# One core, three chained networks: the last block's stage joined with block 3's down product, a re-costed planner, six units' numerators in float32

## Chip, cores and metric

The kernel runs on one NeuronCore of a Trainium2 chip. The metric is the device time of one execution in microseconds; of several runs the median is taken. TensorE (PE) does the matrix products, ScalarE (ACT), VectorE (DVE) and GpSimd (POOL) the elementwise work, SyncE (SP) and ACT issue the DMAs.

## The reference

Everything is float32. B = 4, H = 8, S = 576, D = 64, M = 128 features; 2304 tokens, d_model 512, d_ff 1536; then 8 experts with 4 slots each and a hidden size of 1024.

```python
# 1: attention by random features, for each (b, h)
phi(x) = exp(x @ omega.T - |x|^2/2 - rowmax) / sqrt(M)
kv, z  = phi(k).T @ v, sum_s phi(k)
att    = (phi(q) @ kv) / (phi(q) @ z + 1e-6)       # -> x, 2304 x 512
# 2: gated block
x2  = (sigmoid(x @ w_gate) * (x @ w_val)) @ w_out  # 512 -> 1536 -> 512
# 3: soft mixture of experts
logits = x2 @ phi                                  # 2304 x 32
d = softmax over the tokens; slot_input = d.T @ x2 # 32 x 512
slot_out[e] = relu(slot_input[e] @ w1[e]) @ w2[e]
c = softmax over the slots; out = c @ slot_out
```

## The kernel before, in words

**Tiling.** The heads are taken two at a time: 16 units (`u`), four per batch. The tokens of the gated block are five blocks (`BLOCKS`): blocks 0 to 3 with 512 tokens, the last one (block 4) with the 64 left-over tokens of each batch, 256 in all. d_ff is cut into 12 steps `f` of 128. Products that need more than one float32r pass are made of three: both operands are split into a float32r high part (`hi_of`, a copy) and low part (`lo_of`, a subtract), and `three` (line 464) issues high x high, high x low, low x high. Other products are plain float32 and appear in the trace as two matmul instructions each.

**Stages** (`GROUPS`, and the loop at line 1525): block 0's first six steps beside the units 4 to 7; all of block 1 beside the units 8 to 15; the rest of block 0; blocks 2 and 3 as a pair by a seven-product (Strassen-like) scheme (`pair_jobs`, line 1451), in which block 2's down product runs along and block 3's gated values are kept in `GB`; then block 3's down product alone (the tail of `pair_jobs`, 12 steps: `split_out` splits w_out's tile into w2/ga_a buffers, `late_split` splits `GB[f]`, `downs` issues 12 matmuls); then block 4 (`moe_jobs`, line 1393): for each f `gate` (line 847) 12 matmuls into bank `ga`, Sigmoid on ACT; `val` (line 861) 12 matmuls into bank `va`, a multiply on DVE, a split; `down` (line 880) 12 matmuls into `o0` to `o3`. Each step of block 4 splits three weight tiles of 128x512 (`split_w`, line 819), loaded by SP into the six slots of `WR` (trace name `ws`) from the DRAM scratch `wscr`. So w_out's tiles are loaded and split once for block 3 and once more for block 4.

**The mixture part.** When a block's x2 is done, `moe2_chunks` (line 1107) makes its logits (`chunk_logits`, 32-column matmuls), the running max and sum with Exp on ACT, transposes (`chunk_ltT`, `chunk_cT`) and the slot sums (`chunk_slot`). For the slot sums x2 is needed with tokens on the partitions: `chunk_x2` transposes 32x32 squares on DVE and `chunk_back` (line 1089) writes them into place with 16 DMAs on SP's queue (trace `x2T<-x`). `join_slots` (line 1167) joins the four row groups, `last_slots` (line 1191) adds block 4, then come `layer1` for the eight experts, `layer2` and `combine`. The expert weights (33.5 MB) are loaded into whatever region is free: w1 by `load_w1` (ACT's queue), w2 by `load_w2` (SP's queue).

**Numerators.** `chunk_num` (line 670) multiplies phi(q) by kv. For the units below `N_NUM` = 10 this is plain float32; for the units 10 to 15 kv and the transposed phi(q) are split (`chunk_kv` line 617, `chunk_qT` line 635) and `three` is used, two heads x two halves of 288 columns a unit.

**What sets the order.** Nothing is issued as written. Every operation goes into `Plan` (line 112) with a key in planned microseconds (`plan.t` less a lead by job kind, `LEAD`). The keys come from the constants `SPAN`, `SPANQ`, `SPAND`. `Plan.schedule` (line 248) then runs a list schedule: for each engine the ready operation with the lowest key, with the durations of `Plan.cost` (line 208), a hand-over `HOP` between engines, a DMA model and 1.3 us for a change of ACT's function table. A PSUM tile counts as a whole bank (`span`, line 145). The resulting order is fixed in the program: each engine runs its list in order, and waits where an operand is late. All instructions are issued by line 425 (`issue`), so the trace is read by tile names.

There are eight PSUM banks: `o0` to `o3`, `ga`, `va` and two `fl`. Trace names: `g` = the big staging regions, `XT` = tokens of a block, `gt` = split gated values, `w` = split weights, `more` and `ga_a` = further split buffers, `x` = the tag `x2`.

Of the kernel before, what the change touches and what calls it, by code (L numbers as in the profile page):

```python
# [32 lines left out]
PAIR = (2, 3)  # L33
# [28 lines left out]
N_NUM = 10  # L62
LATE8 = 0.1
FLOOR = 8
WIDE = 15
# [12 lines left out]
SPAN = [88.0, 143.0, 71.0, 45.0]  # L78
SPANQ = 147.0
SPAND = 33.0  # L80
# [5 lines left out]
    "m2": {"PE": 0, "EW": 0},  # L86
    "ex": {"PE": 0.0, "EW": 20.0, "lazy": True},
# [4 lines left out]

SIZE = {F32: 4, F32R: 4, I32: 4, U32: 4, I64: 8}
HOP = 0.16
RELOAD = 1.3
TURN = 0.2
# [5 lines left out]
class Eng:  # L102
# [5 lines left out]
    def __getattr__(self, method):  # L108
        return lambda *a, **k: self.plan.add([(self.name, method, a, k)])


class Plan:
# [95 lines left out]
    def cost(self, eng, method, kw, outs, ins):  # L208


        if method == "together":
# [3 lines left out]
        if eng == "ACT" and method == "dma_start" and o.tensor.name.startswith("out_"):  # L215
            return 0.55, False
# [28 lines left out]
        return 0.6 if eng == "SP" and o.tensor.name.startswith("x2T") and o.ap[0][1] == 32 else 0.06, False  # L245


    def schedule(self):
# [47 lines left out]
        table = 0  # L296
        order = []
# [60 lines left out]
        while ev:  # L358
# [13 lines left out]
            for e in E:  # L372
                while free_at[e] <= now + 1e-9:
# [22 lines left out]
                    want = {AF.Exp: 0, AF.Ln: 0, AF.Sigmoid: 1}.get(alt[3].get("func"), table) if e == "ACT" else table  # L396
                    if want != table:
                        c, table = c + RELOAD, want
                    if held:
                        port = now + c  # L400
                    end = now + c
                    if alt[1] == "dma_start":
# [5 lines left out]
                        end = max(dma, now + nb / 340e3) + 2.0  # L408
# [23 lines left out]
def body(ctx, tc, nc, qkT, tok, von, omT, wall, phi, w1, w2, ident_d, srep_d, rrep_d, mask_d, out):  # L432
# [330 lines left out]
    USE = [(i + (p < 2), p) for i in range(LAST - 1, NS) for p in range(3) if LAST <= i + (p < 2) < NS]  # L763
# [3 lines left out]
    def load_part(k):  # L767
        if todo:
            m = todo.pop(0)
            slot[USE[m]] = k  # L770
            W[USE[m]] = WR[:, k, :]
            SP.dma_start(out=W[USE[m]], in_=wscr[USE[m][0] % NF][:, USE[m][1], :])
# [46 lines left out]
    def split_w(i, part):  # L819
        if i >= NS:  # L820
            return
        end = (i, part) == (NS - 1, 2)
        t = T([128, 2, 512], "w0" if end else f"w{part}", F32R)
        w = W.pop((i, part))
        hi_of(t[:, 0, :], w, SITE["hw"])
        lo_of(t[:, 1, :], w, t[:, 0, :], ("DVE",) if end else SITE["lw"])
        WS[i, part] = t
        if i >= LAST:
            k = slot[i, part]
            if k < 4 or USE.index((i, part)) < WIDE:  # L830
                load_part(k)
            else:
                spent.append(k)
                if len(spent) == 2:
                    free_early()

    def up_passes(i, part, tag):
# [3 lines left out]
        ps = bank(tag)[:, 0:n]  # L841
# [5 lines left out]
    def gate(i):  # L847
        n = BLOCKS[STEPS[i][0]][1]
        ps = up_passes(i, 0, "ga")
        a = T([128, 512], "ga_a", F32, 2)[:, 0:n]  # L850
        if i >= LAST:
# [9 lines left out]
    def val(i, sg):  # L861
        n = BLOCKS[STEPS[i][0]][1]
        ps = up_passes(i, 1, "va")
        if i < LAST:
            gt = T([128, 2, 512], "gt", F32R, 2)
        else:
            if i == LAST:
                G["last"] = T([128, 2, 2, 256], "gt", F32R, 2)
# [139 lines left out]
    def evac_out(j, banks):  # L1008
        n = BLOCKS[j][1]
        x = ms["x2T"] if j == NB - 1 else T([128, 4, 512], "x2T")  # L1010
# [5 lines left out]
        if j == NB - 1:  # L1016
            x = x.rearrange("p k c -> p (k c)")[:, 0:1024].rearrange("p (k c) -> p k c", k=4)
# [4 lines left out]
    def chunk_logits(j):  # L1022
# [7 lines left out]
        lt = T([128, 2, 128], "lt", F32, 2)  # L1030
        mx = T([128, 4], "mx2", F32, 2)
# [62 lines left out]

    def chunk_slot(j):
# [3 lines left out]
        for g in range(ng):  # L1099
            PE.matmul(ps[32 * g:32 * g + 32, :].rearrange("p (c a) -> p c a", a=32), s["dt"][:, 32 * g:32 * g + 32],  # L1100
                      s["x2v"][:, g], start=True, stop=True)
# [5 lines left out]
    def moe2_chunks(j):  # L1107
        back = [lambda h=h: chunk_back(j, h) for h in range(4)]
# [15 lines left out]
    def load_w1():  # L1124

        e = len(W1)
        if e < E:
            W1.append(pieces(EXTAGS[e], 3 if EXTAGS[e] == "XT" else 1))
            for c in range(4):
                ACT.dma_start(out=W1[e][c], in_=w1[e, :, 1024 * c:1024 * c + 1024])  # L1130
# [8 lines left out]
    def free_more():  # L1139

        free.extend(pieces("more", 1, 2))
        plan.floor = plan.t
        load_w2()
        plan.floor = 0.0

    def free_early():

        lead, plan.lead = plan.lead, LEAD["ex"]
        free.append(WR[:, 4:6, :].rearrange("p a c -> p (a c)"))
# [3 lines left out]
    def free_halves():  # L1153

        ms["x2T"], ms["x2"] = T([128, 4, 512], "x2T"), T([128, 4, 512], "x2")
        for x in (ms["x2T"], ms["x2"]):
            free.append(x.rearrange("p k c -> p (k c)")[:, 1024:2048])
        load_w2()

    def free_rest():  # L1160

        w = [WR[:, k:k + 2, :].rearrange("p a c -> p (a c)") for k in (0, 2)]
        free.extend(w[:1] + pieces("w1", 1, 1) + pieces("XT4", 1, 2) + w[1:])
        for tag, bufs in (("w2", 1), ("w0", 1), ("gt", 2)):
# [26 lines left out]
    def last_slots():  # L1191
# [52 lines left out]
        free.extend([x.rearrange("p k c -> p (k c)"), x2[:, 0:2, :].rearrange("p k c -> p (k c)")])  # L1244
# [16 lines left out]
    def layer1(e, si):  # L1261

        ps = bank(("ga", "va")[e % 2])[:, 0:256]
        for k in range(4):
            for g in range(4):
                PE.matmul(ps[32 * g:32 * g + 32, :], si[:, k, :], W1[e][k][:, 256 * g:256 * g + 256],
                          start=k == 0, stop=k == 3)
# [75 lines left out]
    ACT.preload_act_table_set("natural_log_exp_and_others")  # L1343
# [107 lines left out]
    def pair_jobs(t):  # L1451
# [8 lines left out]
        def tiles():  # L1460
            g = region(0, F32)
            h = half_region(0, F32)
            GB.extend(x[:, 512 * k:512 * k + 512] for x, n in ((g, 8), (h, 4)) for k in range(n))
# [34 lines left out]
        t += SPANQ  # L1498
        places = [4, 2, 0, 4, 2, 4]
        dt = SPAND / NF  # L1500
        for n in range(6):
            f, at, t0 = 2 * n, places[n], t + SPAND * n / 6
            if n in (0, 1):
                add(t + 0.2 + 0.1 * n, lambda f=f, at=places[n + 1]: pair_load(f + 2, 2, at))
            add(t0 + 0.02, lambda f=f, at=at: (split_out(f, at), late_split(f)))
            add(t0 + 0.03, lambda f=f, at=at: (split_out(f + 1, at)))
            downs(f, t0 + 0.04 + dt, PAIR[1], "b")
            add(t0 + 0.05 + dt, lambda f=f: late_split(f + 1))
            downs(f + 1, t0 + 0.06 + 2 * dt, PAIR[1], "b")
            nxt = {0: lambda: pair_load(6, 2, 4), 1: lambda: pair_load(8, 2, 2), 3: lambda: pair_load(10, 2, 4),  # L1510
                   2: lambda: (load_part(0), load_part(1)), 4: lambda: (load_part(2), load_part(3)),
                   5: lambda: (load_part(4), load_part(5))}[n]
            add(t0 + 0.035, nxt)
        add(t + SPAND - 6.0, lambda: (split_w(LAST, 0), split_w(LAST, 1)))
        return t + SPAND

    def m2_jobs(j, t, span):
        m2c = moe2_chunks(j)
        jobs.extend((t + span * k / len(m2c), "m2", c) for k, c in enumerate(m2c))
# [5 lines left out]
    for g, (j, f0, f1) in enumerate(GROUPS):  # L1525
        span = SPAN[g]
        if j == NB - 1:
# [3 lines left out]
            jobs += [(start - SPAND + 1.0 + 8 * k, "ex", load_w1) for k in range(4)]  # L1531
            m2_jobs(PAIR[0], start - SPAND + 1.0, SPAND * 0.9)
            m2_jobs(PAIR[1], start + span / NF, span * 0.7)
            jobs += [(start - 5.0, "ex", load_w1), (start + 2.0, "ex", load_w1), (start + 8.0, "ex", free_more),
                     (start + span * 0.9, "end", free_halves), (start + span * 0.85, "m2", join_slots)]
# [10 lines left out]
    jobs += moe_jobs(NS, start, 1.0)  # L1546
# [88 lines left out]
```

## Time and profile before

| | us |
|---|---|
| median of 3 runs | 669.89 (667.93 to 673.65) |
| the profiled execution, whole time | 666.81 |
| its span, first to last instruction | 664.9 |
| PE busy | 644.0 (97%) |
| DVE / ACT / POOL busy | 479.7 / 410.6 / 289.2 |

The span is what the profile's rows divide up; 1.9 us lie around it. The profiled execution is 3.1 us shorter than the median of the three timed runs. "Busy" of PE means that some matmul was under way; as matmuls overlap by a drain of some 0.16 us, the start of one group to the start of the next is the better measure of what a group costs. The TensorE clock was granted in full (1.00, the 2.4 GHz level) in all stretches up to 655 us.

### The profile page before, as it was taken

The page shows a single profiled execution, that of the slowest core. Times are in us where ns is not written, and L with a number is a line of the kernel's source. Part 1 is how long each engine was busy: PE and PEld are TensorE (multiplying, and loading weights), DVE is VectorE, ACT ScalarE, POOL GpSimd, SP SyncE. Part 2 cuts the span into 40 slices and gives each one's busy share as a digit, 9 for nine tenths or more (in the row PEclk, how much of TensorE's full clock was granted, in tenths as well). Part 3 has the DMA queues.
Part 4 walks back from the last instruction along what each step waited for, and adds up shares of the span by engine and source line. Part 5 has one row for each costly group of instructions (what it writes and reads, how often), then busy time and mean ns, then how long its engine had stood idle before and what let it go on. Part 6 is the DMA issues. An engine that isn't in the chain of part 4 may idle for free.

```text
span 664.9 us, 12634 instructions
## 1 busy us (share of the span) xinstructions
PE 644.0 (97%) x4268; PEld 513.2 (77%) x4268; DVE 479.7 (72%) x1379; ACT 410.6 (62%) x937; POOL 289.2 (43%) x272
## 2 busy tenths in 40 slices
PE   7899999999999999999999999999999999899995
PEld 5676777768888888888877778878888779899663
DVE  5898989888998765667689987557557757756323
ACT  4899989889998866777675654534442225445012
POOL 0456344455445344455453555555551453542100
PEclk9999999999999999999999999999999999999998
DMA  7987857678976345223315552222228899777988
GB/s 233 324 269 260 274 188 273 204 237 272 298 260 215 101 115 176 90 97 98 109 49 185 195 147 78 63 64 63 65 65 293 278 316 346 229 233 264 353 334 240
DMA packets 55216, 132.17 MB, mean 199 GB/s; under 512 B 6256, under 2 KB 14192, under 8 KB 55152
## 3 DMA queue, kind: packets, MB, share of 16 engines
q1 hardware_dynamic: 49328, 114.01, 52.7%
q10 hardware_dynamic: 5824, 17.37, 7.7%
q8 instruction: 33, 0.54, 0.3%
q14 instruction: 31, 0.25, 0.1%
HBM read 113.00 MB, written 14.16 MB: 191 GB/s over the span
## 4 chain that ended last, share of the span: by engine, by line
PE 84%; DMA 5%; DVE 4%; ACT 2%; POOL 1%; SPq 1%; issue 1%; DVEq 0%; POOLq 0%; ACTq 0%
PE o L425 24%; PE fl L425 23%; PE va L425 19%; PE ga L425 18%; DMA g<-in_tok 2%; DMA x2T<-x 1%; DMA g<-in_w 1%; DVE g L425 1%; DMA ws<-wscr 1%; SPq L425 1%; DVE XT L425 1%; POOL g L425 1%; DVE ga_a L425 1%; ACT w L425 0%; DMA g<-in_qkT 0%
## 5 line engine op out<-in xcount | busy, mean ns | idle before, releaser
L425 POOL TENSOR_TENSOR w<-ws,w 128x512 fp32r<-128x512 f32 (+1 forms) x101 | 120.6, 1195 | 161.3 <-ACT w L425 67.2
L425 PE MATMUL o<-gt,w 128*128 128x512 f32 (+1 forms) x576 | 134.7, 372 | 2.2 <-POOL w L425 0.9
L425 PEld LDWEIGHTS o<-gt,w 128*128 128x128 f32 x576 | 97.2, 189 | 24.4 <-issue 2.4
L425 PE MATMUL ga<-XT,w 128*128 128x512 f32 (+1 forms) x432 | 101.6, 367 | 0.9 <-POOL XT L425 0.9
L425 ACT ACTIVATE w<-ws 128x512 fp32r<-128x512 f32 (+1 forms) x100 | 57.7, 579 | 72.3 <-PE o L425 28.1
L425 PE MATMUL va<-XT,w 128*128 128x512 f32 (+1 forms) x432 | 100.1, 366 | 1.6 <-DVE ga_a L425 1.1
L425 PE MATMUL fl<-g,g 64*128 64x128 f32 (+4 forms) x686 | 84.1, 313 | 3.5 <-ACT g L425 1.7
L425 ACT ACTIVATE g<-g 128x128 f32<-128x128 f32 (+4 forms) x206 | 73.8, 414 | 16.9 <-DVE g L425 12.9
L425 PEld LDWEIGHTS ga<-XT,w 128*128 128x128 f32 x432 | 69.9, 189 | 16.8 <-issue 4.7
L425 PEld LDWEIGHTS va<-XT,w 128*128 128x128 f32 x432 | 70.5, 189 | 15.2 <-issue 2.4
L425 PEld LDWEIGHTS fl<-g,g 64*128 64x128 f32 (+2 forms) x686 | 60.3, 182 | 24.4 <-issue 7.3
L425 ACT ACTIVATE x2T<-g 128x512 f32<-128x512 f32 x72 | 45.8, 666 | 4.2 <-DVE x L425 2.4
L425 ACT ACTIVATE g1b<-g1b,g 128x128 f32<-128x128 f32 x128 | 40.8, 389 | 5.9 <-DVE g L425 5.7
L425 DVE TENSOR_SCALAR x2T<-x2T 128x512 f32<-128x512 f32 (+1 forms) x72 | 35.9, 513 | 3.7 <-ACT x2T L425 3.4
L425 POOL TENSOR_TENSOR g<-g 128x640 f32<-128x640 f32 (+1 forms) x19 | 23.4, 1230 | 33.3 <-DMA g<-in_tok 13.3
L425 DVE CUSTOM_DVE_ANT_0 g<-fl,g 128x128 f32<-128x128 f32 x142 | 32.3, 286 | 6.5 <-PE fl L425 6.4
L425 PE MATMUL o<-gt,ga_a 128*128 128x512 f32 x144 | 35.4, 393 | 0.0
L425 DVE TENSOR_TENSOR XT<-fl,XT 128x512 f32<-128x512 f32 x24 | 16.6, 690 | 23.0 <-PE fl L425 23.0
L425 POOL TENSOR_TENSOR x<-x2T 128x512 int32<-128x512 int32 x19 | 24.6, 1295 | 16.1 <-DVE x2T L425 11.3
L425 PEld LDWEIGHTS o<-gt,ga_a 128*128 128x128 f32 x144 | 26.7, 188 | 5.8 <-POOL ga_a L425 0.3
L425 ACT ACTIVATE ga_a<-ga_a 128x512 f32<-128x512 f32 x48 | 30.0, 624 | 1.7 <-DVE ga_a L425 1.4
L425 POOL TENSOR_TENSOR w<-x,w 128x512 fp32r<-128x512 f32 x15 | 19.3, 1285 | 24.2 <-DVE x2T L425 11.5
(254 smaller groups left out, 1264.3 us busy)
## 6 DMA issues: line engine op xcount, KB each, us to landing
ws<-wscr SPq DMA_DIRECT2D x42, 512.0 KB, 3.7
g<-in_wall SPq DMA_DIRECT2D x36, 512.0 KB, 5.0
ws<-wscr SPq DMA_DIRECT2D x54, 256.0 KB, 3.7
wscr<-x SPq DMA_DIRECT2D x36, 256.0 KB, 4.6
g<-in_qkT SPq DMA_DIRECT2D x15, 576.0 KB, 5.3
g<-in_tok SPq DMA_DIRECT2D x15, 576.0 KB, 5.1
g<-in_w ACTq DMA_DIRECT2D x16, 512.0 KB, 6.9
XT<-in_w ACTq DMA_DIRECT2D x12, 512.0 KB, 4.6
```

What stands on the lines that cost most here:

```text
L425: ins = getattr(self.eng[e], method)(*a, **k)
```

## The change

Three things are done.

1. **The stages.** Block 3's down product and block 4 become one stage (`tail_jobs`). Step s splits w_out's tile once (`split_t`, part 2) for both; its matmuls go in the order: block 4's val products for f = s-1, block 4's down for f-1, half of block 3's down for s, block 4's gate for f, Sigmoid and multiply, the other half of block 3's down. Val and gate share one bank (`o2`, two halves of 256 columns); block 3 accumulates in `ga`, `va`, `o0`, `o1`, block 4 in `o3` and one `fl`. The last two gates use the Abs/Exp/Ln/Exp form of the earlier stages in place of Sigmoid, and the Exp/Ln table is loaded beforehand. Block 3's slot part comes between its last down product and the end of block 4; its x2 is transposed by PE (`turn_block`, 16 transposes into four banks, four copies) and no longer by DVE and 16 DMAs. The loads of w1 and w2 move with the memory: w1 of experts 6 and 7 goes piece by piece into the regions of `GB`, half of expert 7's only after block 4's x2 has been read.
2. **The planner.** Durations, hand-over and DMA costs are replaced (factors in `PACE`, 0.15 us in `SWITCH` when the matmul's shape goes to or from less than 128 rows or columns, issue costs for SP's and ACT's DMAs), and the keys are stretched by 4%.
3. **Numerators.** `N_NUM` = 16: the units 10 to 15 use plain float32 too; their splits of kv and phi(q) go.

```diff
-N_NUM = 10
+N_NUM = 16
-SPAN = [88.0, 143.0, 71.0, 45.0]
-SPANQ = 147.0
-SPAND = 33.0
+SPAN = [91.5, 148.7, 73.8, 46.8]
+SPANQ = 152.9
+SPAND = 34.3
+LAG = 1
+M3 = 6.0
+M2 = 45.0
+W1S = [1.0, 8.0, 15.0, 22.0, 24.0, 36.0, 50.0, 63.0, 29.0]
+TAIL0, TAIL1 = 2.75, 4.2
-HOP = 0.16
+HOP = 0.2
-TURN = 0.2
+PACE = {"PE": 1.006, "ACT": 1.03, "DVE": 1.04, "POOL": 1.03}
+SWITCH = 0.15
+LAND = 2.3
+TURN = 0.0
...
+    def split_t(f, part):
+        if part == 2:
+            t = OB[f % 3]
+        else:
+            t = T([128, 2, 512], f"w{part}", F32R)
+        w = WR[:, slot[f, part], :]
+        hi_of(t[:, 0, :], w, SITE["hw"])
+        lo_of(t[:, 1, :], w, t[:, 0, :], SITE["lw"])
+        WS[LAST + f, part] = t
+        if slot[f, part] < 5:
+            load_part(slot[f, part])
...
-        ps = bank(tag)[:, 0:n]
+        if i < LAST:
+            ps = bank(tag)[:, 0:n]
+        elif i < NS - 2:
+            if part == 1:
+                G["up"] = bank("o2")
+            ps = G["up"][:, n * part:n * part + n]
+        else:
+            ps = bank(("o2", "ga")[part])[:, 0:n]
...
-        if i >= LAST:
+        if LAST <= i < NS - 2:
             ACT.activation(out=a, in_=ps, func=AF.Sigmoid)
             return a
...
+    def turn_block(j, g):
+        x = ms[j]["x2T"]
+        ps = bank(("va", "o0", "o1", "va")[g])
+        for k in range(4):
+            PE.transpose(ps.rearrange("p (i k a) -> p k i a", i=4, k=4)[:, k], x[:, k, 128 * g:128 * g + 128], ident)
+        copy(ms[j]["y"][g], ps, (("ACT", "DVE"), ("DVE", "ACT"))[g % 2])
...
+    def tail_jobs(t):
...
+        for s in range(NF + LAG + 1):
+            f = s - LAG
+            if s < NF:
+                add(t - 0.5, lambda s=s: split_t(s, 2))
+                add(t - 0.4, lambda s=s: late_split(s))
+            if s == NF - 1:
+                add(t, lambda: down_b(NF - 1, range(4)))
+                t += TAIL0
+                add(t, lambda: (evac_out(PAIR[1], banks[2]), turn_places()))
+                m2_jobs(PAIR[1], t + 0.2, M3, "m3")
+                add(t + 0.25 + M3, free_gt, "end")
+                add(t + 0.3 + M3, join_slots, "m3")
+            if f in (NF - 2, NF - 1):
+                add(t - 0.3, lambda f=f: split_t(f, 0))
+                add(t, lambda f=f: G.__setitem__("s", gate(LAST + f)))
+                add(t + 0.3, lambda f=f: split_t(f, 1))
+                t += TAIL1 / 3
+                add(t, lambda f=f: G.__setitem__("val", up_passes(LAST + f, 1, "")))
+                add(t + 0.01, lambda f=f: val(LAST + f, G.pop("s")))
+                t += TAIL1 / 3
+            elif 0 <= f < NF:
+                add(t - 0.3, lambda f=f: split_t(f, 1))
+                add(t, lambda f=f: G.__setitem__("val", up_passes(LAST + f, 1, "")))
+                add(t + 0.3, lambda f=f: split_t(f, 0))
+                t += TAIL1 / 3
+            if 0 <= f - 1:
+                add(t, lambda f=f: down_c(f - 1))
+                t += TAIL1 / 3
...
+            if s < NF - 1:
+                add(t, lambda s=s: down_b(s, (0, 1)))
+                t += TAIL0 / 2
+            if 0 <= f < NF - 2:
+                add(t, lambda f=f: val(LAST + f, gate(LAST + f)))
+                t += TAIL1 / 3
+            if s < NF - 1:
+                add(t, lambda s=s: down_b(s, (2, 3)))
+                t += TAIL0 / 2
+        return t
...
+            jobs += [(start + W1S[4 + c], "ex", lambda c=c: load_w1(W1[6], (c,))) for c in range(4)]
+            jobs.append((start + W1S[8], "ex", lambda: load_w1(W1[7], (2, 3))))
...
-        free.extend([x.rearrange("p k c -> p (k c)"), x2[:, 0:2, :].rearrange("p k c -> p (k c)")])
+        load_w1(W1[E - 1], (0, 1))
```

`down_b` and `down_c` issue 3 matmuls for each of four column tiles, like `down` before, with 512 and 256 columns.

## Rows read from the trace of the kernel before

**Rows 1.** The page: busy time of each engine and its share of the span.

```profile
PE 644.0 (97%) x4268; PEld 513.2 (77%) x4268; DVE 479.7 (72%) x1379; ACT 410.6 (62%) x937; POOL 289.2 (43%) x272
```

**Rows 2.** Busy time by stretch: engines with counts, PE clock, DMA share, GB/s.

```profile
20.00:40.00 20.00, 17.79 (x111) 13.28 (x110) 19.37 (x96) 18.88 (x56) 10.22 (x9) 1.00 0.79 265
60.00:80.00 20.00, 18.41 (x106) 13.38 (x107) 19.29 (x60) 19.34 (x47) 10.96 (x11) 1.00 0.82 282
340.00:400.00 60.00, 59.04 (x290) 46.28 (x289) 53.97 (x95) 37.05 (x72) 29.17 (x33) 1.00 0.49 152
508.35:611.40 103.05, 99.99 (x698) 87.39 (x696) 71.10 (x147) 40.39 (x68) 45.57 (x33) 1.00 0.84 280
```

**Rows 3.** The timeline of PE: start, us, operation, count, idle before.

```profile
511.07 2.88 PE L425 MATMUL o<-gt,ga_a 128*128 128x512 f32 x12
513.79 2.88 PE L425 MATMUL o<-gt,w 128*128 128x512 f32 x12
516.60 1.08 PE L425 MATMUL fl<-x2T,phs 128*32 128x128 f32 x32
517.61 3.01 PE L425 MATMUL o<-gt,ga_a 128*128 128x512 f32 x12
...
538.41 2.56 PE L425 MATMUL o<-gt,w 128*128 128x512 f32 x10 [0.46 <-DVE w L425]
...
564.29 1.60 PE L425 MATMUL ga<-XT,w 128*128 128x256 f32 x12
565.73 1.60 PE L425 MATMUL va<-XT,w 128*128 128x256 f32 x12
...
573.07 1.22 PE L425 MATMUL o<-gt,w 128*128 128x256 f32 x8 [0.73 <-POOL w L425]
...
576.79 0.50 PE L425 MATMUL va<-XT,w 128*128 128x256 f32 x2 [1.06 <-DVE ga_a L425]
577.81 1.44 PE L425 MATMUL va<-XT,w 128*128 128x256 f32 x10 [0.51 <-POOL w L425]
```

**Rows 4.** The timeline of SP's queue and ACT around the stalls at 573 to 578.

```profile
572.94 2.42 SPq L425 DMA_DIRECT2D x2T<-x  x3
575.46 1.03 SPq L425 DMA_DIRECT2D ws<-wscr  x2
...
577.40 0.63 ACT L425 ACTIVATE w<-ws 128x512 fp32r<-128x512 f32 x1 [5.91 <-DMA ws<-wscr]
```

**Rows 5.** Groups by form: matmuls of the numerators, units 10 to 15, then 8 and 9.

```profile
L425 PE MATMUL fl<-g 128*128 128x288 f32 x72 | 11.5, 295 | 0.0
...
L425 PE MATMUL fl<-g,g 128*128 128x288 f32 x16 | 4.5, 404 | 0.0
```

**Rows 6.** The timeline from block 4's logits to its slot sums.

```profile
612.43 0.66 PE L425 MATMUL fl<-ident,x2T 128*128 128x128 f32 x4
613.02 0.27 PE L425 MATMUL o<-ident,lt 64*128 64x64 f32 x1
613.74 1.28 ACT L425 ACT_TABLE_LOAD   x1
614.24 0.22 DVE L425 TENSOR_TENSOR dt<-o,cs 128x64 f32<-128x64 f32 x1
615.03 0.26 ACT L425 ACTIVATE dt<-dt 128x64 f32<-128x64 f32 x1
```

**Rows 7.** The timeline of one undisturbed gate and val of block 4, all engines.

```profile
601.26 1.60 PE L425 MATMUL va<-XT,w 128*128 128x256 f32 x12
601.47 0.38 ACT L425 ACTIVATE ga_a<-ga 128x256 f32<-128x256 f32 x1 [0.81 <-PE ga L425]
...
602.96 0.63 ACT L425 ACTIVATE w<-ws 128x512 fp32r<-128x512 f32 x1 [1.11 <-PE va L425]
602.98 0.42 DVE L425 TENSOR_TENSOR ga_a<-va,ga_a 128x256 f32<-128x256 f32 x1 [1.03 <-PE va L425]
...
603.65 0.68 DVE L425 TENSOR_TENSOR w<-ws,w 128x512 fp32r<-128x512 f32 x1
```

More of the change, by code (lines that the diff above doesn't have):

```diff
@@ L208, in cost, with base @@
     def cost(self, eng, method, kw, outs, ins):
+        c, held = self.base(eng, method, kw, outs, ins)
+        return c * (1.0 if method == "together" else PACE.get(eng, 1.0)), held
+    def base(self, eng, method, kw, outs, ins):
         if method == "together":
@@ L214, in cost @@
         n = self.free(o) if o is not None else 0
-        if eng == "ACT" and method == "dma_start" and o.tensor.name.startswith("out_"):
-            return 0.55, False
+        if eng == "ACT" and method == "dma_start":
+            return 0.42, False
         if eng == "PE":
@@ L296, in schedule @@
         table = 0
+        form = None
         order = []
@@ L395, in schedule @@
                     c, held = self.cost(e, alt[1], alt[3], outs, ins)
-                    want = {AF.Exp: 0, AF.Ln: 0, AF.Sigmoid: 1}.get(alt[3].get("func"), table) if e == "ACT" else table
+                    want = 0 if alt[1].startswith("preload") else {AF.Exp: 0, AF.Ln: 0, AF.Sigmoid: 1}.get(alt[3].get("func"), table) if e == "ACT" else table
                     if want != table:
                         c, table = c + RELOAD, want
+                    if e == "PE":
+                        o, x = (outs[0], ins[0]) if alt[1] != "together" else [y[0] for y in alt[3]["parts"][0][1:]]
+                        last, form = form, min(o.ap[0][1], x.ap[0][1]) < 128
+                        c += SWITCH * (last != form)
                     if held:
@@ L1030, in chunk_logits @@
         lt = T([128, 2, 128], "lt", F32, 2)
+        if j == PAIR[1]:
+            plan.place([("ACT", "preload_act_table_set", (EXP_LN,), {})], [lt[0:p, 0, :], WR[:, 5, 0:256]], [WR[:, 5, 256:512]])
         mx = T([128, 4], "mx2", F32, 2)
@@ L1107, in moe2_chunks @@
     def moe2_chunks(j):
+        if j == PAIR[1]:
+            turns = [lambda g=g: turn_block(j, g) for g in range(4)]
+            return [lambda: chunk_logits(j)] + turns + [lambda: chunk_ltT(j), lambda: chunk_slot(j), lambda: chunk_cT(j)]
         back = [lambda h=h: chunk_back(j, h) for h in range(4)]
@@ L1122, in pieces, with load_w1 @@
         return [t[:, 1024 * c:1024 * c + 1024] for c in range(n)]
[L1124 to L1130, printed above, removed]
+    def load_w1(x=None, cs=range(4)):
+        if x is None:
+            e = len(W1)
+            x = pieces(EXTAGS[e], 3 if EXTAGS[e] == "XT" else 1)
+            W1.append(x)
+        e = next(k for k, y in enumerate(W1) if y is x)
+        for c in cs:
+            ACT.dma_start(out=x[c], in_=w1[e, :, 1024 * c:1024 * c + 1024])
     def load_w2():
@@ L1514, in pair_jobs, with buffers, late_split, down_b @@
-        add(t + SPAND - 6.0, lambda: (split_w(LAST, 0), split_w(LAST, 1)))
-        return t + SPAND
-    def m2_jobs(j, t, span):
+        return t + SPANQ
+    OB = []
+    def tail_jobs(t):
+        add = lambda at, f, name="moe": jobs.append((at, name, f))
+        def buffers():
+            m = T([128, 2, 2, 512], "more", F32R)
+            OB.extend([m[:, 0], m[:, 1], T([128, 2, 512], "w2", F32R)])
+            slot.update({(0, 2): 4, (1, 2): 5})
+            y = T([128, 2, 512], "gt", F32R, 2)
+            x = [T([128, 512], "ga_a", F32R, 2) for _ in range(2)]
+            G["late"] = (y[:, 0], y[:, 1]), x
+            ms["x2T"], ms["x2"] = G["h"], G["h"][:, 1024:2048].rearrange("p (g c) -> p g c", g=2)
+            G["last"] = T([128, 2, 2, 256], "gt", F32R, 2)
+        def late_split(f):
+            gt = G["late"][f % 2]
+            hi_of(gt[0], GB[f], SITE["hg"])
+            lo_of(gt[1], GB[f], gt[0], SITE["lg"])
+        def down_b(f, ks):
+            if f == 0 and ks[0] == 0:
+                banks[2] = [bank(x) for x in ("ga", "va", "o0", "o1")]
+            w, g = WS[LAST + f, 2], G["late"][f % 2]
+            for k in ks:
+                c = slice(128 * k, 128 * k + 128)
+                three(banks[2][k], (w[:, 0, c], w[:, 1, c]), g, f == 0, f == NF - 1)
+        def down_c(f):
+            if f == 0:
+                banks[1] = [bank("o3"), bank("fl")]
+            w, g = WS.pop((LAST + f, 2)), G.pop(LAST + f)
+            for k in range(4):
+                c = slice(128 * k, 128 * k + 128)
+                ps = banks[1][k // 2][:, 256 * (k % 2):256 * (k % 2) + 256]
+                three(ps, (w[:, 0, c], w[:, 1, c]), (g[:, 0, 0:256], g[:, 1, 0:256]),
+                      f == 0 and k % 2 == 0, f == NF - 1, True)
+        def turn_places():
+            y = T([128, 2, 512], "gt", F32, 2)
+            G["y"] = y
+            ms[PAIR[1]]["y"] = [y[:, 0], y[:, 1]] + [T([128, 512], "ga_a", F32, 2) for _ in range(2)]
+        add(t - 0.6, buffers)
+        add(t - 0.50 * SPANQ / 6, lambda: (load_part(0), load_part(1)))
+        add(t - 0.1 * SPANQ / 6, lambda: (load_part(2), load_part(3)))
+        for s in range(NF + LAG + 1):
[26 more added lines that the diff above has]
+                t += TAIL1 / 3
+                if f == NF - 1:
+                    add(t, free_more, "end")
+            if s < NF - 1:
[8 more added lines that the diff above has]
+        return t
@@ L1530, in body @@
             start = pair_jobs(start)
[L1531 to L1535, printed above, removed]
+            jobs += [(start + W1S[k], "ex", load_w1) for k in range(4)]
+            jobs += [(start + W1S[4 + c], "ex", lambda c=c: load_w1(W1[6], (c,))) for c in range(4)]
+            jobs.append((start + W1S[4] - 0.01, "ex", big_regions))
+            jobs.append((start + W1S[8], "ex", lambda: load_w1(W1[7], (2, 3))))
+            jobs.append((start + M2 + W2S, "ex", free_x2))
+            m2_jobs(PAIR[0], start + 1.0, M2)
+            start = tail_jobs(start)
+            continue
         for f in range(f0, f1):
```

111 lines of the change are left out of this document (50 added, 61 removed).

## The prediction

> **What bounds the kernel now.** I read the page first, then the busy time by stretch, then the timeline of the stage that is rebuilt, then the groups by form, and last the two places where one engine hands to the next. The page shows PE busy for 97% of the span, DVE for 72%, and the others less [rows 1]. So the time is the sum of PE's instructions plus the places where PE waits, and those are few. The stretches show where: 2.21 us without a matmul in 20 to 40 us, 1.59 in 60 to 80, 0.96 in 340 to 400, and 3.06 in the 103.05 us of block 3's down product and block 4 together [rows 2]. A change of the order can win back no more than such waits, and what PE gets in addition is paid in full.
>
> A busy PE is not a PE at its peak, so for the rebuilt stage I count from start to start. A group of twelve 512-column matmuls takes 513.79 - 511.07 = 2.72 us, one of 256 columns 565.73 - 564.29 = 1.44 us [rows 3]. The stage from 508.35 to 611.40 holds 14 groups of the first kind (two still belong to block 2) and 36 of the second: 38.1 + 51.8 = 89.9 us. That leaves 13.2 us for the mixture part's insertions and for stalls. A block's logits cost about 1.2 us (from 516.51, where the group before was due to end, to 517.61, and a late second matmul behind it) [rows 3]. Two logits, two slot sums, the joining of the slots and the small transposes are some six such insertions, estimated at 7.2 us. So up to 6.0 us are stalls. Four of them stand in the rows: 0.46, 0.73, 1.06 and 0.51 us idle, each with 0.16 us of drain that a full pipeline hides (1.60 - 1.44), 3.4 us in all [rows 3].
>
> Their cause is visible too. PE waits for weights split on POOL, or for the multiply on DVE. Behind that is SP's queue: the writes of block 3's x2 (three in 2.42 us) stand ahead of two weight loads at 575.46, and ACT's split starts at 577.40 after 5.91 us of waiting for its load [rows 4].
>
> **The change part by part.**
>
> *Joined stage: the stalls.* Block 4's steps become longer (three groups of 1.44 us with one of 2.72 us, about 7.0 us in place of 4.3), with the same three weight splits in them. Twelve loads and twelve splits of w_out go, and so do block 3's 16 DMAs on SP's queue. Everything that is late in rows 3 and 4 gets more time. What is late next is the hand-over of the shared bank, below. The ends are 0 (the stalls stay) and -6.0 us; I take the middle of the shown 3.4 and the 6.0: **-4.7 us**.
>
> *Joined stage: PE's turns.* The 16 transposes that replace DVE's and the 16 DMAs are new work for PE. Four such transposes take 613.02 - 612.43 = 0.59 us [rows 6], so sixteen 2.4 us. The other end is 0, if PE would wait there for block 3's softmax anyway; a gain is excluded, since they are added to the bound engine. I take **+2.4 us**.
>
> *The shared bank.* In the old stage the gate writes bank `ga`, val writes `va`. Now both halves lie in `o2`, and the next step's val may start only when this step's multiply has read the bank. From the start of the group behind a gate, Sigmoid begins 0.21 us later and lasts 0.38; the multiply begins 0.12 us after its releaser (602.98 against 602.86) and lasts 0.42; the same 0.12 back to PE gives 1.25 us [rows 7]. The cover is half of block 3's group, six matmuls, 1.36 us. The margin is 0.11 us in each of ten steps. In front of Sigmoid can stand a split of 0.63 us, in front of the multiply a subtract of 0.68 us [rows 7], so the worst step is 0.63 + 0.68 - 0.11 = 1.2 us late, ten of them 12 us. The lower end is 0: block 3's matmuls wait only for splits, which are made long ahead, so the list can put them in between, one by one. That it does so as planned is likelier, since both engines are under 70% busy there (71.10 and 40.39 of 103.05 us [rows 2]); I take **+0.5 us**.
>
> The Trainium skill speaks against using the halves as two buffers: on the page "PSUM — Partial Sum Buffer", section "PSUM bank collisions raise a hardware error", two engines must not touch one bank at once, whatever columns they touch. By that rule every step has the hand-over counted above; if halves were free of each other, the term would be 0 and the sum 0.5 us less. The old trace keeps gate and val in two banks and so cannot show which.
>
> *The last two gates* trade Sigmoid for Abs, Exp, Ln, a DVE operation and Exp: four operations of 0.38 and one of 0.42 us in place of one of 0.38, 1.56 us longer [rows 7]. The first has val, a down group and block 3's insertions beside it. The last has val and one down group, 2.88 us, against 0.21 + 1.94 + five hand-overs of 0.12 + 0.42 = 3.2 us to the end of its multiply, and a split of that behind it. Ends 0 and 2 x 1.56 = 3.1 us; I take the uncovered rest, **+0.5 us**. In return the table is already right behind block 4: now Exp of `dt` starts at 615.03 though its operand is ready at 614.46, behind a load of 1.28 us [rows 6]. Ends 0 and -1.28; I take the shown wait less a hand-over, **-0.5 us**.
>
> *Numerators.* Units 8 and 9 have 8 products in 4.5 us, 0.563 each; the units 10 to 15 have 24 in 11.5 us, 0.479 each [rows 5]. Twenty-four products in float32 cost 24 x 0.084 = **+2.0 us** on PE. The splits that go were on DVE and ACT, which hold nothing up in the stretch of these units, so they give nothing back; the ends are 0 (they take the place of a wait) and 2.0.
>
> *Late loads.* Half of expert 7's w1 is loaded only after block 4's x2 is read. Seven experts are multiplied first, so I cost it at nothing; without that cover 1 MB at the stage's 280 GB/s [rows 2] is 3.7 us. The pieces of w1 in the regions of `GB` are issued by ACT; if one is issued before its region is free, the Sigmoid queued behind it waits, and PE with it, as in the shared bank's case.
>
> *The planner elsewhere.* Nothing in the trace says what the new order will be. PE's waits before the joined stage are 2.21 + 1.59 + 0.96 = 4.8 us [rows 2]. A plan with better durations can remove them at most, and a worse order can add as much: -4.8 to +4.8. I take half of the gain, **-2.4 us**, since these waits are places where the engines came later than the old plan held. Stretching all keys alike moves no key past another.
>
> **The sum.** -4.7 + 2.4 + 0.5 + 0.5 - 0.5 + 2.0 - 2.4 = -2.2 us. On the profiled execution, 666.81 us, that gives 664.6; the median of the runs shown lies 3.1 us above that execution, so the forecast is 667.7 us against 669.89, no change within the 1% that a measurement of this kernel can tell.
>
> **The rivals.**
>
> *The bank decides (slower).* Splits stand ahead of Sigmoid and multiply in most steps, and PE has no block 3 matmul left to put in. It decides from the point where the multiply ends more than 1.36 us after the gate. At 12 us in place of 0.5 the time is 664.6 + 11.5 + 3.1 = 679.2. For it: the margin is 0.11 us; against: PE's list holds ready matmuls.
>
> *Everything fits (faster).* The joined stage loses all 6.0 us, the turns lie in block 3's softmax wait, the bank and the gates cost nothing, and the planner removes all 4.8: -6.0 - 0.5 + 2.0 - 4.8 = -9.3, or 660.6 us. For it: the idle causes in rows 3 and 4 are all relieved; against: it needs every term at its end.
>
> *The stalls stay (the joining does not do what it says).* DMA is busy for 0.84 of the old stage [rows 2]. If the loads of w1 keep the weights late, the 4.7 us are not won: 667.7 + 4.7 = 672.4 us. For it: ACT waited for a load, not for POOL [rows 4]; against: 3 MB of loads and the x2 writes go.
>
> **How the numbers follow.** Forecast 0.42 (between 664 and 672 us), everything fits 0.27, the stalls stay 0.18, the bank decides 0.13. Faster by over 1% means under 663.2 us: 0.27 and 0.03 from the forecast's lower end, 0.30. Slower by over 1%, above 676.6 us: 0.13 and 0.01, 0.14. The rest, 0.56, is within 1%. The range of 659 to 676 us holds the faster case and the case of the staying stalls, and leaves out most of the bank's case.
>
> **What would show it.** In the profile after: no matmul group of 256 columns in the joined stage preceded by idle time; the stage with its turns at some 101 us; 16 transposes of about 0.15 us; 48 float32 instructions of 288 columns more, and none in threes; no table load between block 4's logits and its slot sums. Idle time of PE released by DVE ahead of an `o2` group, ten times, would show the bank's case; idle time released by a load of `ws` the staying stalls. A large change of PE's idle time before 500 us would mean that the planner, which I could only bound, was the main part, and the forecast wrong.

## The result, and the profile after

The changed kernel is slower: 677.48 us (median of 20 runs, 671.13 to 683.06) against 668.69 us (20 runs). The ratio is 1.0112, 95% interval 1.0091 to 1.0132, some 7.5 us; it is taken over the runs in the faster of two states alone and is not the quotient of the medians. The forecast was 667.7 us and no change, and the range ended at 676.

The profiled execution has a span of 676.1 us, 11.2 us more than the one before. That is more than the ratio gives: the one before was 1.9 us faster than its kernel's median, this one is 0.6 us slower than its own. A stage's figure below is that of one such execution. First the busy time by stretch: the pair stage, the joined stage, the tail (us of the stretch, then PE, PEld, DVE, ACT, POOL with counts, PE clock, DMA share, GB/s).

```profile
360.48:509.72 149.24, 149.24 (x681) 120.04 (x679) 103.27 (x177) 70.13 (x143) 75.54 (x89) 1.00 0.38 114
509.72:622.62 112.90, 104.07 (x714) 90.81 (x712) 56.88 (x127) 43.58 (x72) 37.20 (x30) 0.97 0.65 209
622.62:676.10 53.48, 45.49 (x817) 30.82 (x816) 18.10 (x62) 7.56 (x25) 1.90 (x2) 0.96 0.92 333
```

And of the kernel before the stretches that [rows 2] doesn't have; the stage from 508.35 us stands there:

```profile
0.00:357.33 357.33, 348.87 (x2077) 275.10 (x2078) 288.57 (x1001) 291.73 (x699) 165.22 (x148) 1.00 0.60 195
357.33:508.35 151.02, 150.06 (x681) 119.94 (x679) 102.38 (x175) 69.58 (x145) 76.50 (x89) 1.00 0.36 111
...
611.43:664.90 53.47, 45.04 (x816) 30.81 (x815) 17.65 (x60) 8.86 (x27) 1.90 (x2) 0.97 0.89 316
```

Everything up to the pair takes 360.48 us in place of 357.33 (+3.2), the pair 149.24 in place of 151.02 (-1.8), the tail is the same to 0.1 us. The loss is the joined stage: 112.90 in place of 103.05 [rows 2], +9.8 us, with 8.8 us without a matmul and a mean clock of 0.97. POOL and DVE have less to do there, as meant. So the work went and the waits grew.

The waits of PE, longest first (total, times, longest):

```profile
PE o L450 <- DVE ws L450: 6.6, 3, 4.2
PE fl L450 <- DVE g L450: 2.8, 4, 0.9
PE fl L450 <- ACT lt L450: 2.2, 1, 2.2
```

The first and the third lie in the joined stage, and no other wait does. The first is the hand-over of the shared bank (`o`), which waits for the multiply on DVE (`ws` is the buffer of Sigmoid's result now). But it happens three times and not ten, so I followed it back. The timeline of the first two follows, without POOL and weight loads; rows with SPq and ACTq are DMA issues, and brackets give the engine's idle time before a row and what ended it:

```profile
532.16 6.81 SPq L450 DMA_DIRECT2D x2T<-x  x8
...
534.04 0.34 ACTq L450 DMA_DIRECT2D g<-in_w  x1
...
534.40 1.28 ACT L450 ACT_TABLE_LOAD   x1 [3.49 <-DMA x2T<-x]
535.70 0.38 ACT L450 ACTIVATE ws<-o 128x256 f32<-128x256 f32 x1
...
536.12 0.43 DVE L450 TENSOR_TENSOR ws<-o,ws 128x256 f32<-128x256 f32 x1 [2.73 <-ACT ws L450]
...
536.60 1.70 PE L450 MATMUL o<-XT,w 128*128 128x256 f32 x12 [2.00 <-DVE ws L450]
...
539.07 1.56 SPq L450 DMA_DIRECT2D ws<-wscr  x3
...
542.48 0.33 SPq L450 DMA_DIRECT2D x<-in_w  x1
...
542.86 6.33 SPq L450 DMA_DIRECT2D ws<-wscr  x3
...
546.68 0.43 DVE L450 CAST w<-ws 128x512 fp32r<-128x512 f32 x1 [5.54 <-DMA ws<-wscr]
...
547.56 0.41 DVE L450 TENSOR_TENSOR ws<-o,ws 128x256 f32<-128x256 f32 x1
...
548.02 2.21 PE L450 MATMUL o<-XT,w 128*128 128x256 f32 x12 [4.17 <-DVE ws L450]
```

Read upward from each PE row. At 536.60 PE waits for the multiply, that for Sigmoid, and Sigmoid stands on ACT behind a table load and a DMA issue of w1. ACT did nothing for 3.49 us, and by the profile what ended that was the landing of one of the 16 writes of block 2's x2. At 548.02 the multiply on DVE stands behind a split that waits 5.54 us for its weights. That load was issued at 542.86, after SP had worked through eight of the same writes. Three weight loads had gone out in between, but then SP waited for a write to land before it could issue a load of w2 into `x`, the region that the writes read:

```profile
SPq L450 <- DMA x2T<-x: 1.7, 1, 1.7
```

The weight load stood behind that w2 load in SP's queue. The groups behind the second wait then run at a lower clock, and so do those at the end of the stage:

```profile
547.00:553.00 6.00, 4.97 (x29) 4.98 (x30) 3.34 (x6) 0.81 (x2) 3.84 (x3) 0.72 0.84 318
612.00:618.00 6.00, 4.64 (x24) 3.04 (x25) 2.34 (x10) 3.11 (x8) 0.73 (x1) 0.72 0.51 175
```

A mean granted clock of 0.72 over six microseconds means that part of them ran at the 1.2 GHz level, half of full speed; (1 - 0.72) x 6.00 is some 1.7 us lost each time. Before each fall PE had waited: 4.17 us, and 2.23 us after 0.43. The second place is the end of the stage, here ACT with the two PE rows behind a wait:

```profile
607.06 0.41 ACT L450 ACTIVATE ws<-ws 128x256 f32<-128x256 f32 x1
607.49 1.28 ACT L450 ACT_TABLE_LOAD   x1
...
608.78 0.51 ACT L450 ACTIVATE ws<-ws,one_b 128x256 f32<-128x256 f32 x1
...
609.80 1.33 PE L450 MATMUL o<-XT,w 128*128 128x256 f32 x9 [0.43 <-DVE ws L450]
609.83 1.28 ACT L450 ACT_TABLE_LOAD   x1
...
611.12 0.42 ACT L450 ACTIVATE ws<-ws 128x256 f32<-128x256 f32 x1
611.55 1.28 ACT L450 ACT_TABLE_LOAD   x1
612.85 0.37 ACT L450 ACTIVATE lt<-fl,mx 128x128 f32<-128x128 f32 x1
...
613.36 0.44 PE L450 MATMUL fl<-ident,lt 128*128 128x128 f32 x2 [2.23 <-ACT lt L450]
```

The gate of step 10 runs Exp, then loads a table, Ln, loads a table, Exp; only then comes the load that was meant to spare all this. It is issued inside block 3's `chunk_logits`, and its job is sorted behind the job of that gate, whose buffer it claims as written. So it cannot go ahead of it.

Added up: 89.9 us of matmuls and 7.2 of insertions, as in the prediction (the second an estimate), 2.4 for the transposes, 8.8 of waits, some 0.2 of drain at each of the three long ones, and 3.4 for the clock make 112.3 of the 112.9 us.

### The profile page after: what moved, and what is told of

It reads as the page before. It is cut to its first block, busy times and chain, and to the rows that moved or that the text cites. A ratio compares the mean times of both kernels' runs of the same rounds, so it can differ in the third digit from the quotient of the medians.

```text
span 676.1 us, 12474 instructions
## 1 busy us (share of the span) xinstructions
PE 649.7 (96%) x4260; PEld 516.6 (76%) x4260; DVE 463.8 (69%) x1356; ACT 409.1 (61%) x934; POOL 262.9 (39%) x259
## 4 chain that ended last, share of the span: by engine, by line
PE 84%; DMA 5%; DVE 4%; ACT 3%; SPq 1%; issue 1%; POOL 0%; DVEq 0%; POOLq 0%
PE o L450 25%; PE fl L450 24%; PE va L450 19%; PE ga L450 17%; DMA g<-in_w 2%; DVE g L450 2%; ACT g L450 1%; SPq L450 1%; DVE x2T L450 1%; DMA ws<-wscr 1%; DMA g<-in_von 1%; DMA g<-in_tok 1%; DVE ga_a L450 0%; ACT L450 0%; ACT x2T L450 0%
## 5 line engine op out<-in xcount | busy, mean ns | idle before, releaser
L450 PE MATMUL o<-gt,w 128*128 128x512 f32 (+1 forms) x396 | 103.5, 398 | 0.0
L450 PE MATMUL ga<-XT,w 128*128 128x512 f32 (+1 forms) x312 | 86.3, 405 | 0.7 <-DVE ga_a L450 0.7
L450 PEld LDWEIGHTS o<-gt,w 128*128 128x128 f32 x396 | 71.9, 190 | 17.3 <-DVE gt L450 2.0
L450 PE MATMUL va<-XT,w 128*128 128x512 f32 x288 | 80.8, 409 | 0.0
L450 PEld LDWEIGHTS ga<-XT,w 128*128 128x128 f32 x312 | 55.9, 192 | 16.7 <-issue 4.8
L450 PEld LDWEIGHTS va<-XT,w 128*128 128x128 f32 x288 | 52.4, 188 | 13.7 <-issue 2.6
L450 PE MATMUL o<-XT,w 128*128 128x256 f32 x264 | 37.2, 289 | 6.6 <-DVE ws L450 6.6
L450 POOL TENSOR_TENSOR g<-g 128x512 f32<-128x512 f32 (+1 forms) x23 | 26.1, 1133 | 43.4 <-DVE g L450 20.2
L450 PEld LDWEIGHTS o<-XT,w 128*128 128x128 f32 x264 | 35.1, 194 | 9.0 <-DVE ws L450 7.7
L450 DVE SCALAR_TENSOR_TENSOR x2T<-g,x2T 128x512 int32<-128x512 int32 x36 | 29.1, 816 | 0.1
```

The source lines that it names most:

```text
L450: ins = getattr(self.eng[e], method)(*a, **k)
```

## The experiments

Ratios are to the kernel before on the same chip, with 95% intervals; the kernel after stands at 1.0112. Every edit gives a new list for all engines, so a run also changes the order in places that its edit does not name.

### Each part by itself

Four kernels divide the change. The numerators alone:

```diff
-N_NUM = 10
+N_NUM = 16
```

> The kernel before with N_NUM = 16 alone. Theory: TensorE bounds these units, so the 24 products cost their 0.084 us each and the time rises by 2.0 us (ratio about 1.003), with fewer DVE splits giving nothing back. Rival (the numerators carry the loss): the ratio is 1.008 or more.

Measured: 1.0002 (0.9975 to 1.0029). Neither number is met; a loss of 2.0 us lies just outside the interval. The float32 group costs what the rows said:

```profile
L425 PE MATMUL fl<-g,g 128*128 128x288 f32 x64 | 18.1, 405 | 0.0
```

The 64 instructions take 18.1 us, where 16 took 4.5 and the 72 in threes 11.5 [rows 5], +2.1. The profile has the pair stage starting 1.34 us later (358.67) and ending only 0.77 later: the 0.96 us that PE waited in 340 to 400 us [rows 2] is gone.

```profile
358.67:509.12 150.45, 150.39 (x681) 119.80 (x679) 101.93 (x171) 70.65 (x146) 77.34 (x89) 1.00 0.36 113
```

The planner alone (class `Plan`, its constants and the stretched keys of the kernel after, the body of the kernel before):

```diff
-SPAN = [88.0, 143.0, 71.0, 45.0]
...
+SPAN = [91.5, 148.7, 73.8, 46.8]
...
-HOP = 0.16
+HOP = 0.2
...
+PACE = {"PE": 1.006, "ACT": 1.03, "DVE": 1.04, "POOL": 1.03}
...
```

> The kernel before with the new durations, hand-over, DMA costs and stretched keys alone; stages and numerators as before. Theory: the new order is not what costs; the pair's stage gets some 1.8 us shorter as in the kernel after, the first stages stay within 1.5 us, so the ratio is 0.996 to 1.001. Rival (the new plan carries the loss): 1.008 or more.

Measured: 1.0035 (1.0006 to 1.0064), 2.3 us slower: outside both expectations. The new order is itself a small loss in the old stages. In the profile the first stages are 1.7 us longer, the pair 0.7, and the two old stages 5.1; this execution took 675.36 us, 3.0 more than its kernel's median, so the stages are overstated:

```profile
510.73:618.86 108.13, 102.46 (x699) 88.04 (x697) 67.52 (x138) 44.11 (x75) 46.70 (x35) 0.98 0.79 261
```

The joined stage alone, under the old plan (the old class `Plan`, its constants, the old keys and numerators):

```diff
-N_NUM = 16
+N_NUM = 10
...
-SPAN = [91.5, 148.7, 73.8, 46.8]
...
+SPAN = [88.0, 143.0, 71.0, 45.0]
...
```

> The joined stage with the old durations, old keys and N_NUM = 10. Theory: the loss sits in the joined stage, where weight loads and an ACT queue wait behind block 2's writes of x2 and where table loads stand in the chain of the last gates; both are there under either plan, so 5 to 10 us slower than before (1.007 to 1.015), with idle time of PE released by DVE ahead of o2 groups. Rival (the new plan puts them there): at most 1.003.

Measured: 1.0068 (1.0038 to 1.0098), just under the theory's 1.007 and clear of the rival's 1.003. The larger part of the loss is here, without the new plan, and PE waits at the same two kinds of place:

```profile
PE o L437 <- DVE ws L437: 3.9, 3, 1.9
PE fl L437 <- ACT lt L437: 1.7, 1, 1.7
```

The numerators undone in the kernel after:

```diff
-N_NUM = 16
+N_NUM = 10
```

> The kernel after with N_NUM = 10 (the numerators undone). Theory: 2 us shorter than the kernel after, so 1.008 of the kernel before; the joined stage keeps its waits. Rival (the numerators carry the loss): 1.000 to 1.003.

Measured: 1.0103 (1.0063 to 1.0144), as the kernel after within the uncertainty. My 2 us did not show here either, but these are four runs, and the interval holds the 1.008 too.

### The two causes in the joined stage

The table load moved ahead of the gate:

```diff
-        if j == PAIR[1]:
-            plan.place([("ACT", "preload_act_table_set", (EXP_LN,), {})], [lt[0:p, 0, :], WR[:, 5, 0:256]], [WR[:, 5, 256:512]])
...
+        def table_first():
+            plan.place([("ACT", "preload_act_table_set", (EXP_LN,), {})], [WR[:, 5, 0:256]], [WR[:, 5, 256:512]])
...
-                add(t, lambda: (evac_out(PAIR[1], banks[2]), turn_places()))
+                add(t, lambda: (table_first(), evac_out(PAIR[1], banks[2]), turn_places()))
```

> The kernel after, with the load of the Exp/Ln table placed ahead of the gate of step 10 and not behind it. Theory: the three table loads inside that gate's chain and the wait of 2.2 us behind them go, and the half clock that followed with them: 3 to 4.5 us shorter than the kernel after (ratio 1.005 to 1.008), two or three table loads fewer. Rival (the shared bank alone delays val): less than 1 us, ratio 1.010 to 1.012.

Measured: 671.89 us, ratio 1.0014 (0.9983 to 1.0045): more than expected came back. One table load stands at 597.17 and none behind it; the wait for `lt` is gone, the waits at the bank are not, and a wait for a split on ACT (`more`) stands beside them:

```profile
PE o L450 <- DVE ws L450: 4.5, 2, 3.2
...
PE ga L450 <- ACT more L450: 1.2, 1, 1.2
```

The joined stage is 3.3 us shorter by it, and its clock still falls:

```profile
508.29:617.88 109.59, 103.55 (x714) 90.67 (x713) 58.20 (x128) 39.83 (x70) 37.24 (x30) 0.97 0.67 214
```

The fall at the end of the stage is gone, but the one behind the longest wait at the bank, 3.2 us here, cost more than before, some 2.7 of these 5.4 us:

```profile
546.64:552.00 5.36, 5.36 (x25) 5.36 (x26) 2.37 (x2) 0.63 (x1) 3.40 (x3) 0.50 0.85 316
```

Of the 6.6 us between the ratios only half is thus seen in the stage. The stage starts 1.4 us earlier, in an order that is new there too; what is left is within the two intervals.

Block 2's writes left out. The kernel then makes block 2's slot sums from x2 that was never turned, so it shows only what the writes cost in time:

```diff
+        if j == PAIR[0]:
+            return [lambda: chunk_logits(j), lambda: chunk_x2(j), lambda: chunk_ltT(j), lambda: chunk_cT(j), lambda: chunk_slot(j)]
```

> The kernel after without the 16 DMAs that write block 2's transposed x2 into place (block 2's slot sums are then made from x2 not turned). Theory: ACT's w1 load and SP's weight loads no longer wait behind these writes, so both waits ahead of o2 groups (2.0 and 4.2 us) and the half clock behind the second go: 6 to 8 us shorter than the kernel after (ratio 0.999 to 1.003). Rival (the shared bank with its 0.11 us of margin makes the waits): they stay, ratio above 1.008.

Measured: 669.59 us, ratio 0.9994 (0.9969 to 1.0019). The waits of PE from 500 to 620 us are now these, and that is all of them:

```profile
PE fl L450 <- ACT lt L450: 2.2, 1, 2.2
PE o L450 <- DVE ws L450: 0.4, 1, 0.4
PE o L450 <- DVE lt L450: 0.2, 1, 0.2
```

The bank is still shared and the 6.6 us are 0.4; the table's 2.2 us stay. So the two causes are separate, and the single bank alone is not one of them.

Block 2 turned by TensorE, with nothing left out:

```diff
+            turns = [lambda g=g: turn_first(j, g) for g in range(4)]
+            return [lambda: chunk_logits(j)] + turns + [lambda: chunk_ltT(j), lambda: chunk_slot(j), lambda: chunk_cT(j)]
```

> The kernel after with block 2's x2 turned by TensorE too: 16 transposes in place of DVE's and the 16 DMAs, nothing left out. Theory: as without the writes, less 2.4 us for the transposes: 4 to 6 us shorter than the kernel after (ratio 1.002 to 1.006). Rival (shared bank): 2 us longer than the kernel after, 1.014.

Measured: 671.41 us, ratio 1.0023 (1.0000 to 1.0046), as expected.

Both mends, and the numerators undone:

```diff
-N_NUM = 16
+N_NUM = 10
...
+        def table_first():
...
+            turns = [lambda g=g: turn_first(j, g) for g in range(4)]
```

> The kernel after with block 2 turned by TensorE, the table loaded ahead of the gate of step 10, and N_NUM = 10. Theory: 4.5, 4 and 2 us off the kernel after, some 667 us, ratio 0.996 to 1.000. Rival (the joined stage is bound by its single bank): 1.006 or more.

Measured: 666.21 us, ratio 0.9948 (0.9920 to 0.9975), faster than both kernels, the point a little below the theory's 0.996. The joined stage:

```profile
508.37:610.38 102.01, 101.67 (x731) 89.86 (x729) 56.10 (x129) 39.82 (x70) 35.99 (x29) 1.00 0.65 219
```

It takes 102.0 us, though it has 2.4 us of transposes more than the kernel after; PE's busy time falls short of it by 0.34 us only, and the mean clock is 1.00.

### ACT's queue or SP's

The 16 writes made both ACT's w1 load and SP's weight loads late. To part the two I kept the writes and the early table, and let SP issue w1 of the experts 2 to 7:

```diff
-            ACT.dma_start(out=x[c], in_=w1[e, :, 1024 * c:1024 * c + 1024])
+            (ACT if e < 2 else SP).dma_start(out=x[c], in_=w1[e, :, 1024 * c:1024 * c + 1024])
```

> As preload_first, with the w1 loads of the experts 2 to 7 issued by SP in place of ACT. Theory: ACT's queue no longer stands still behind a w1 load that waits for a write of block 2's x2 to land, so the waits of 1.2 us each ahead of an o2 and of a ga group (534 and 541 us in preload_first) go; SP's own lateness, the 3.3 us wait at 547, stays or grows. Ratio 0.998 to 1.001 against 1.0014 for preload_first. Rival (only the lateness of SP's weight loads counts): the two short waits stay and the ratio is 1.001 to 1.004.

Measured: 667.46 us, ratio 0.9989 (0.9965 to 1.0012). The ratio is the theory's, but the wait that should have stayed is 0.8 us. From 500 to 620 us PE waits for `ws` just once, and the second fence is the joined stage:

```profile
PE o L450 <- DVE ws L450: 0.8, 1, 0.8
```

```profile
509.20:610.84 101.64, 100.46 (x715) 88.36 (x713) 56.50 (x126) 41.48 (x73) 36.02 (x29) 1.00 0.70 230
```

The writes are all there. With w1 among SP's own issues the plan spreads them, one or two at a time, with loads between, where before eight writes stood in a row:

```profile
531.17 0.51 SPq L450 DMA_DIRECT2D x2T<-x  x1
...
531.77 0.53 SPq L450 DMA_DIRECT2D ws<-wscr  x1
...
532.34 0.52 SPq L450 DMA_DIRECT2D x2T<-x  x1
...
532.96 0.53 SPq L450 DMA_DIRECT2D ws<-wscr  x1
```

So this run shows that the writes alone, in this order, do no harm, not that ACT's queue alone did it.

The two mends, early table and turns, with the numerators left in float32 and the new plan:

```diff
+        def table_first():
...
+            turns = [lambda g=g: turn_first(j, g) for g in range(4)]
```

> The kernel after with block 2 turned by TensorE and the table loaded early, numerators left in float32 (all_three without its N_NUM = 10). Theory now: float32 numerators cost TensorE some 2 us before the pair stage and give about 1 us back at its start (no wait for the split of the pair's tokens), so within 1.5 us of all_three: ratio 0.994 to 0.998. Rival (2.0 us, as predicted, nothing back): 0.998 or more.

Measured: 667.28 us, 0.9988 (0.9961 to 1.0014). The point lies on the rival's side by 0.1%, the interval covers both.

The same with the old class `Plan`, its constants and keys, and the old numerators:

```diff
-N_NUM = 16
+N_NUM = 10
...
-SPAN = [91.5, 148.7, 73.8, 46.8]
...
+SPAN = [88.0, 143.0, 71.0, 45.0]
...
-HOP = 0.2
+HOP = 0.16
...
```

> The joined stage with both mends, but the old durations and keys and N_NUM = 10. Theory: with no wait on writes and tables the joined stage is bound by TensorE under either plan, some 102 us, and the old plan's first stages are 1 to 3 us shorter (planner_alone was 1.0035): ratio 0.990 to 0.995. Rival (the joined stage needs the new durations): 0.997 or more, with waits ahead of o2 groups.

Measured: 665.40 us, 0.9953 (0.9936 to 0.9970), 3.1 us faster than before on the same chip and without the new durations. It and all_three, 0.9948, cannot be told apart. The point lies a hair above the theory's 0.995, and PE has no wait between the joined stage's first matmul and its last, though ACT still waits once behind a load, 4.4 us at 520.95. So with both mends the joined stage does not need the new plan. Against two_fixes, with which it shared a chip, plan and numerators together are worth 0.35%. As all_three, with the new plan, is as fast as this one, that points to the numerators; but the chips differ, and the numerators alone cost the kernel before nothing measurable, so which of the two it is stays open.

Last, the early table and w1 on SP under the old plan, its keys and numerators:

```diff
-            ACT.dma_start(out=x[c], in_=w1[e, :, 1024 * c:1024 * c + 1024])
+            (ACT if e < 2 else SP).dma_start(out=x[c], in_=w1[e, :, 1024 * c:1024 * c + 1024])
...
-HOP = 0.2
+HOP = 0.16
...
```

> As w1_on_sp, but with the old durations and keys and N_NUM = 10: table early, w1 of the experts 2 to 7 on SP, block 2 turned by DVE and the 16 writes as before. Theory: ACT's standing still behind w1 loads is what makes the waits, under any plan, so the joined stage stays near 101 to 103 us, and the sixteen transposes of two_fixes_old_plan are saved: ratio 0.991 to 0.996. Rival (the new plan's DMA costs are what keeps SP's weight loads in time): waits ahead of o2 groups and a ratio of 0.998 or more.

Measured: 667.03 us, 0.9969 (0.9948 to 0.9990), between the two expectations, with one wait left:

```profile
PE o L437 <- DVE ws L437: 1.8, 1, 1.8
```

So SP's loads are placed a little worse here, by this one wait. Whether the old DMA costs do that, or the keys and durations that go with them, was not parted.

## Why the prediction was wrong, point by point

**The joined stage, -4.7 us: this step failed.** The terms of this stage add up to -1.8 us; it measured +9.8 as a whole. The part on PE's work was right: 89.9 us of groups, the insertions and 2.4 us of transposes give 99.5, "some 101 us" with small waits, and the mended kernels under the new plan measure 101.6 to 102.0. What was wrong is "everything that is late in rows 3 and 4 gets more time". I had read that block 3's x2 writes on SP made the weights late [rows 4], and credited the change with their removal. I did not ask where block 2's 16 writes go: in the kernel before they lie beside block 3's down product, from here to 537 us, with one weight tile a step:

```profile
521.83 4.18 SPq L425 DMA_DIRECT2D x2T<-x  x4
```

Now they lie in the stage that splits three weight tiles in 7 us. With them removed, the waits at the bank fell from 6.6 to 0.4 us.

**ACT's queue: named, and costed at nothing.** The prediction said that a w1 load that has to wait holds up the Sigmoid behind it, "and PE with it". That is the first wait: the gate's matmuls are done at 531.81, and Sigmoid starts at 535.70. I expected it for a region not yet free; the profile shows it ended by the landing of a write of block 2's x2, which has no region in common with it. Why a load of w1 waits for such a write was not tried by itself.

**The table, -0.5 us: the sign was wrong in this place.** At the slot sums of block 4 the load is gone, as forecast. But the load that replaced it stands behind the gate of step 10. So there are two loads inside the chain that I had costed at +0.5, and a third ahead of block 3's softmax, for which PE waits 2.23 us. That was to be seen in the listing: the gate's job is entered at t, the logits' job at t + 0.2, and the preload claims the gate's buffer. Moving the load ahead of the gate took the ratio from 1.0112 to 1.0014.

**The rival of the shared bank** had the right sign and the right row (idle time ahead of `o` groups, released by DVE), and a wrong mechanism. It was to cost 1.2 us in each of ten steps. It was paid three times, each time because ACT or DVE was held up elsewhere, and with nothing held up it cost nothing: the small margin was enough. An undisturbed step of the kernel after shows it, six matmuls of block 3 between gate and val and no idle time:

```profile
588.40 1.59 PE L450 MATMUL o<-XT,w 128*128 128x256 f32 x12
...
589.82 1.56 PE L450 MATMUL o<-ga_a,more 128*128 128x512 f32 x6
...
590.44 0.43 DVE L450 TENSOR_TENSOR ws<-o,ws 128x256 f32<-128x256 f32 x1
...
591.22 1.60 PE L450 MATMUL o<-XT,w 128*128 128x256 f32 x12
```

The rule of the Trainium skill's page "PSUM — Partial Sum Buffer", section "PSUM bank collisions raise a hardware error", could not be tried here. The plan itself counts a tile as a whole bank and makes val wait for the multiply, and a run in which the halves were used freely was not made.

**The stalls stay.** This rival named the mechanism, weights late behind other DMAs, and gave it only the return of 4.7 us. It did not have the clock: two falls cost some 3.4 us, which no term of the sum held.

**The numerators, +2.0 us:** right on PE (+2.1), but measured at 0.0 (up to +1.9) in the time of the kernel before. There the lower end, "they take the place of a wait", was the better half of the bound: a wait of 0.96 us in the pair stage went. Beside the mended stage it may be otherwise: two_fixes, with float32 numerators, is at 0.9988, and all_three, without, at 0.9948.

**The planner, -2.4 us:** wrong by its sign; alone it costs 2.3 us. Of the 3.2 us that the kernel after loses ahead of the pair, the profiles show 1.7 with the planner alone and 1.3 with the numerators alone. That the pair stage loses a wait is due to the numerators.

## What to carry to other kernels

When a stage is pulled together, list for each in-order queue (SP's, and ACT's where it issues DMAs) what will now stand in front of the loads and the activations that the bound engine waits for; the bound engine's own work adds up well, its waits do not. Keep DMA issues that can wait off an engine whose next instruction is on the bound engine's path, and place a table load by the order of the operations that use it, not by where it reads well. A stage that comes out long by waits is not refuted: with two small mends this one is level with the kernel before (0.9988), and with the numerators undone as well it is 0.5% faster.

## What the runs showed of the hardware

A wait of PE can cost more than itself. After a wait of 4.17 us, and after waits of 0.43 and 2.23 us close together, the granted clock fell to the 1.2 GHz level for a while (0.72 on average over six microseconds), so that twelve 256-column matmuls took 2.2 us in place of 1.6 and some 1.7 us were lost each time. After 2.00 us alone, at 536.60, it stayed at 1.00 up to 540 us. The loss does not follow the wait's length alone: in preload_first a wait of 3.2 us, not long after one of 1.2, was followed by 0.50 over 5.4 us, 2.7 us lost. It also differs between executions of one kernel: of the kernel after, the run of 671.13 us has a mean clock of 0.997, that of 681.03 us one of 0.989.

A table load took 1.28 us in every place, also the two between the functions of one gate (607.49 and 609.83). And ACT did nothing for 3.49 us around a DMA issue that itself took 0.34.
